# Gated linear attention and a feed-forward block on one core: three-chunk groups against units of two chunks throughout, with other paths for the rotated rows and the raw weights

## The chip, the cores and the metric

The kernel runs on one core of a Trainium2 chip. A core has a matrix engine (TensorE, "PE"; its weight loads are listed apart as "PEld"), three engines for elementwise work (VectorE "DVE", ScalarE "ACT", GpSimd "POOL"), a synchronisation engine (SyncE, "SP") that here only issues DMA transfers, and 16 DMA engines. Each engine works off its own queue of instructions in order; semaphores order the queues against each other. Matrix products land in PSUM, a separate memory; the rest of the on-chip data lies in SBUF, 128 partitions wide.

The metric is the device time of one execution in microseconds. "Span" is the time from the first to the last instruction in the profile of one execution.

## The reference

Inputs are q, k, v and complex gates `a_re + i a_im`, each of 4 batches, 8 heads, 768 steps, 48 features, then the weights of a feed-forward block. Cut to what matters:

```python
mag = sqrt(a_re**2 + a_im**2)
scale = minimum(mag, 0.999) / (mag + 1e-6)
a = (a_re + 1j*a_im) * scale
for t in range(768):                     # a state of 48 x 48 for each batch and head
    S = a[t][:, None] * S + outer(k[t], v[t])
    y[t] = q[t] @ S.real
x = y, heads side by side                # 3072 tokens x 384
xn = x / sqrt(mean(x*x) + 1e-6) * rms_g
out = (silu(xn @ w_gate) * (xn @ w_val)) @ w_out   # 384 -> 1536 -> 384
```

The weights arrive as 64-bit floats, and the kernel reads them as pairs of 32-bit words and narrows them to 32 bits itself. All products are in 32-bit floats.

## The kernel before

The 3072 tokens are 24 *chunks* of 128 steps, six to a batch. Two chunks are a *unit* (12 units); three chunks are a *group* of the feed-forward block (8 groups).

**Gates, by unit.** `gates(u)` works on tiles of 128 partitions x 768 (three blocks of 128 features by 256 steps). It takes magnitude and angle of the gates, multiplies the magnitudes up along each chunk with a scan (`p`), adds up the angles with another (`re`), takes sine (`s`) and cosine (`y`), and multiplies k by 1/p and q by p, and both by cosine and sine. The four products go into one tile `rot`. The features lie as (d, h), eight heads inside each of the 48 features, so that one head's 96 rows (48 cosine, 48 sine) are spread over the partitions. To gather them, each chunk's slice of `rot` is written to a DRAM tile `way` and read back as `kq`, 96 partitions by heads and steps (lines 629 and 631). The chunk's last decay rides along as a 129th column.

**Attention, by chunk.** `scores(n)`: eight score products `s_ps`, which VectorE masks into `am` (line 723), and eight transposes `kt_ps`, which ScalarE copies to `kt`. `finish(n)`: the state product `state_ps` and its update, the outputs `y_ps` (from `am` and v, and from q and the state before), then the norm: ScalarE squares y (line 761), VectorE scales the sum (`ssq`), GpSimd raises it to -1/2 (`rs`, line 765), ScalarE scales y to `xn` (line 767), TensorE transposes it (line 774), and VectorE writes `xT`.

**Feed-forward, by group.** For each of 12 slices of 128 hidden features: three products for gate, three for value, 384 tokens wide (line 792), Silu on ScalarE, the product `hT` on VectorE. Then for each chunk 12 products with `wo` (line 803), a copy `ot` and a DMA out.

**Weights.** There are 18 parts of 128 x 768 values: 12 of `wg` and `wv`, six of `wo`. Each is fetched raw (768 KB, line 659, on SP's queue; three buffers for the early parts, two for the others) and narrowed by one ScalarE and six VectorE operations.

**What sets the order.** The program is written as generators that are stepped by hand: while `scores` and `finish` of a chunk advance, `run(x, fill)` steps the feed-forward of the group before (the *filler*) and the gates of the unit ahead. The gate and value slices step the narrowing that they need. A list scheduler then puts the instructions of each engine's queue in an order, by their place in the program and by when it expects their inputs, and adds the semaphores; pools with few buffers make a writer wait for the readers of the buffer's last content. In the resulting order of TensorE, a chunk in the middle of the kernel stands as: 8 `s_ps`, 6 gate or value, 8 `kt_ps`, 6 gate or value, 8 `state_ps`, 16 `y_ps`, 12 gate or value, 3 `xT_ps`, 12 gate or value (hardware passes for the feed-forward are counted two to a program matmul in the profile; these are the program's).

The driver's core:

```python
for n in range(N + 1):
    ...                               # every second chunk: start gates of the unit ahead
    if n < N:
        run(scores(n), 1)
    if n > 0:
        run(finish(n - 1), 2)
    if n % GC == 0 and n:
        for _ in filler:
            pass
        ...
        filler = feed_forward(n // GC - 1, pieces, ffn)
```

Of the kernel before, what the change touches and what calls it, by code (L numbers as in the profile page):

```python
# [28 lines left out]
P = 128  # L29
# [442 lines left out]
def fast(tc, ctx, qT, kT, v, a_re, a_im, w_gate, w_val, w_out, rms_g, out, H, bad):  # L472
# [10 lines left out]
    GC = 3  # L483
# [6 lines left out]
    assert NCH % GC == 0 and NCH % UC == 0 and DM % P == 0 and D2 <= P and L * ND == D  # L490
# [23 lines left out]
    def load_gates(u):  # L514
        b, c = divmod(u * UC, NCH)
        t = UN[u]
        for name, ap in (("re", a_re), ("im", a_im)):
            t[name] = prep.tile([P, ND, T], FP32, tag=name, name=name, bufs=2)
            rows = ap[b].rearrange("(h j l) s -> j l h s", j=ND, l=L)
            queue = nc.scalar if u == 0 and name == "im" else nc.sync  # L520
            for j in range(ND):
                queue.dma_start(out=t[name][:, j], in_=rows[j][:, :, c * C:c * C + T])
        for name, ap in (("k", kT), ("q", qT)):
            t[name] = prep.tile([P, ND, T], FP32, tag=name, name=name)
            for i in range(UC):
                nc.sync.dma_start(
                    out=t[name][:, :, i * C:(i + 1) * C],
                    in_=ap[u * UC + i].rearrange("d (h t) -> (d h) t", t=C)
                                      .rearrange("(j p) t -> p j t", p=P))
        for n in range(u * UC, (u + 1) * UC):  # L530
            U[n]["v"] = unit.tile([C, H, D], FP32, tag="v", name="v", bufs=4)
            nc.sync.dma_start(out=U[n]["v"].rearrange("t h d -> t (h d)"),
                              in_=v[n * C:(n + 1) * C, :])

    rot = consts.tile([P, 4 * ND, UC, C + 1], FP32, name="rot")
    nc.vector.memset(rot[:, :, :, C:], 0.0)
    load_gates(0)

    zeros = consts.tile([P, T], FP32, name="zeros")
    nc.gpsimd.memset(zeros, 0.0)
# [17 lines left out]
    def gates(u):  # L560
# [4 lines left out]
        s, w, y, r, p = (prep.tile([P, ND, T], FP32, tag=x, name=x)  # L565
                         for x in ("s", "w", "y", "r", "p"))
# [29 lines left out]
        nc.vector.tensor_copy(  # L596
            out=rot[:, 2 * ND:, :, C].rearrange("p (a j) c -> p a j c", j=ND),
            in_=ends[:, u].unsqueeze(1).to_broadcast([P, 2, ND, UC]))
# [12 lines left out]
        for j in range(ND):  # L611
            nc.vector.tensor_tensor_scan(
                out=re[:, j], data0=im[:, j], data1=zeros, op0=ALU.add, op1=ALU.add,
                initial=UN[u - 1]["turn"][:, j] if u * UC % NCH else 0.0)
# [8 lines left out]
        for i, (x, f) in enumerate(((k, y), (k, s), (q, y), (q, s))):  # L623
            tt(rot[:, i * ND:(i + 1) * ND, :, 0:C], by_chunk(x), by_chunk(f))
        yield
        for i in range(UC):
            n = u * UC + i
            way = dram.tile([4 * DM, C + 1], FP32, tag="way", name="way")
            nc.sync.dma_start(out=way.rearrange("(r p) t -> p r t", p=P), in_=rot[:, :, i])
            to = unit.tile([D2, 2, H, C + 1], FP32, tag="kq", name="kq", bufs=3)  # L630
            nc.sync.dma_start(out=to.rearrange("d x h t -> d x (h t)"),
                              in_=way.rearrange("(x d h) t -> d x (h t)", x=2, h=H))
            U[n]["k"], U[n]["q"] = to[:, 0, :, 0:C], to[:, 1, :, 0:C]
            U[n]["decay"] = to[:, 1, :, C:]
        yield
# [10 lines left out]
    wg = consts.tile([P, ND, DF], FP32, name="wg")  # L646
    wv = consts.tile([P, ND, DF], FP32, name="wv")
# [5 lines left out]
    FW = 2 * P  # L653
    narrowed = [0]
    EARLY = 3

    def fetch(pool, to, src):
        raw = pool.tile([P, to.shape[1], 2 * to.shape[2]], I32, tag="raw", name="raw")
        nc.sync.dma_start(out=raw, in_=src)
        return raw  # L660

    def narrow(stage, to, raw):

        rows, cols = to.shape[1:]
        n = rows * cols
        words = raw.rearrange("p c f -> p (c f)").rearrange("p (n two) -> p n two", two=2)
        lo, hi = words[:, :, 0], words[:, :, 1]
        t, g = (stage.tile([P, n], I32, tag=x, name=x, bufs=1) for x in ("t", "g"))
        as_to = lambda x: x.rearrange("p (c f) -> p c f", f=cols)

        nc.scalar.activation(out=to, in_=as_to(hi.bitcast(FP32)), func=AF.Square)
        stt(as_to(g.bitcast(FP32)), to, (1.125 * 2.0 ** -15) ** 2, as_to(hi.bitcast(FP32)), ALU.is_ge)

        nc.vector.tensor_scalar(out=t, in0=g, scalar1=3, scalar2=0x3FFFFFFF,
                                op0=ALU.logical_shift_left, op1=ALU.bitwise_and)
        stt(t, g, -2 ** 30, t, ALU.bitwise_and, ALU.bitwise_or)

        nc.vector.tensor_scalar(out=g, in0=t, scalar1=-2 ** 23, scalar2=None, op0=ALU.bitwise_and)
        stt(to, as_to(lo.bitcast(U32)), 2.0 ** -52, as_to(g.bitcast(FP32)), ALU.mult)
        tt(to, as_to(t.bitcast(FP32)), to, ALU.add)  # L680

    def load_weights(early, stage):

        parts = []
        for f in range(0, DF, FW):
            parts += [(to[:, :, f:f + FW], ap, slice(0, ND), f) for to, ap in ((wg, w_gate), (wv, w_val))]
# [25 lines left out]
    def scores(n):  # L712
# [3 lines left out]
        am = u["am"] = unit.tile([C, H, C], FP32, tag="am", name="am")  # L716
        hh = H // 2
        for a in range(2):
# [4 lines left out]
            nc.vector.tensor_tensor(out=am[:, a * hh:(a + 1) * hh], in0=ps, op=ALU.mult,  # L723
# [4 lines left out]
        kt = u["kt"] = unit.tile([C, H, D2], FP32, tag="kt", name="kt")  # L728
        for a in range(2):
# [3 lines left out]
            nc.scalar.copy(out=kt[:, a * hh:(a + 1) * hh], in_=ps)  # L733
        yield

    def finish(n):
# [4 lines left out]
        if n % NCH < NCH - 1:  # L741
            ps = ps_a.tile([D2, H, D], FP32, tag="a", name="state_ps")
            for h in range(H):
                nc.tensor.matmul(ps[:, h], lhsT=u["kt"][:, h], rhs=vv[:, h], start=True, stop=True)  # L744
# [9 lines left out]
        for h in range(H):  # L754
            nc.tensor.matmul(ps[:, h], lhsT=am[:, h], rhs=vv[:, h], start=True, stop=prev is None)  # L755
# [3 lines left out]
        x = act.tile([C, DM], FP32, tag="x", name="x", bufs=1)  # L759
        ssq = act.tile([C, 1], FP32, tag="ssq", name="ssq")  # L760
        nc.scalar.activation(out=x, in_=y, func=AF.Square, accum_out=ssq)  # L761
# [4 lines left out]
        xn = act.tile([C, DM], FP32, tag="xn", name="xn")  # L766
# [13 lines left out]
    def feed_forward(g, pieces, ffn):  # L780
        xT = G[g]["xT"]
        hT = ffn.tile([P, NF, GT], FP32, tag="hT", name="hT", bufs=1)
        for f in range(NF):
            fs = slice(f * P, (f + 1) * P)
            if f * P % FW == 0:
                while narrowed[0] < 2 * (f * P // FW + 1):
                    next(pieces)
            gp = ps_g.tile([P, GT], FP32, tag="g", name="gate_ps")
            vp = ps_g.tile([P, GT], FP32, tag="g", name="val_ps")
            for p_, w_ in ((gp, wg), (vp, wv)):  # L790
                for d in range(ND):
                    nc.tensor.matmul(p_, lhsT=w_[:, d, fs], rhs=xT[:, d], start=d == 0,  # L792
                                     stop=d == ND - 1)
            sg = ffn.tile([P, GT], FP32, tag="sg", name="sg")
            nc.scalar.activation(out=sg, in_=gp, func=AF.Silu)  # L795
            tt(hT[:, f], vp, sg)
            yield
        for _ in pieces:
            pass
        for i in range(GC):  # L800
            ps = ps_g.tile([C, DM], FP32, tag="g", name="out_ps")
            for f in range(NF):
                nc.tensor.matmul(ps, lhsT=hT[:, f, i * C:(i + 1) * C], rhs=wo[:, f],  # L803
                                 start=f == 0, stop=f == NF - 1)
                if f == NF // 2:
                    yield
# [4 lines left out]
            yield  # L811


# [4 lines left out]
    for _ in gates(0):  # L818
        pass
    load_gates(1)  # L820
    filler = iter(())
    ahead = iter(())

    def run(x, fill):
        for _ in x:
            for _ in range(fill):
                next(filler, None)
            next(ahead, None)

    behind = None  # L830
    for n in range(N + 1):
        if n % UC == 0 and n // UC + 1 < NU:
            for _ in ahead:
                pass
            if n // UC + 2 < NU:
                load_gates(n // UC + 2)
            ahead = gates(n // UC + 1)
        if n % UC == 0 and n // UC + 1 == NU:
            for _ in ahead:
                pass  # L840
        if n < N:
            run(scores(n), 1)
        if n > 0:
            run(finish(n - 1), 2)
        if n % GC == 0 and n:
            for _ in filler:
                pass
            if n == GC:
                for _ in range(EARLY):
                    next(pieces)  # L850
                first.close()
                ffn = ctx.enter_context(tc.tile_pool(name="ffn", bufs=2))
            filler = feed_forward(n // GC - 1, pieces, ffn)

    ne = NU * ND * UC
    ok = act.tile([P, DM], FP32, tag="x", name="ok", bufs=1)[:, 0:2 * ne + NU]
# [12 lines left out]
    for _ in filler:  # L869
        pass  # L870
# [49 lines left out]
```

## Time and profile before

| What | Value |
| --- | --- |
| Median of 3 runs | 885.33 us (876.48 to 890.41) |
| Profiled execution | 884.13 us, span 882.3 us |
| TensorE busy | 773.3 us (88%), mean granted clock 0.939 |
| VectorE busy | 426.8 us (48%) |
| ScalarE busy | 356.2 us (40%) |
| GpSimd busy | 23.2 us (3%) |
| DMA | 81.17 MB, 36% of the 16 engines' time on SP's queue |
| First score product | 48.8 us after the start |
| TensorE's waits for `kq` from `way` | 77.3 us in 5 waits |

Busy time is the union of an engine's instructions. TensorE's overlap in a pipeline, so the distance between the starts of neighbouring matmuls says what one costs, not its listed duration. The granted clock is the share of TensorE's full clock that the throttle allowed. In the tables of groups, "idle before" is how long the engine stood still ahead of those instructions, and what ended it.

### The profile page before, as it was taken

Reading aid. Unit: us, or ns where it says so; the run is one execution under the profiler, and the core shown is the slowest. Engines: PE = TensorE matmul, PEld = TensorE weight load, DVE = VectorE, ACT = ScalarE, POOL = GpSimd, SP = SyncE. Lnnn points to the kernel's source line nnn. Section 1 sums busy time; section 2 is a strip of 40 time slices with the busy share of each in tenths; the row PEclk is TensorE's granted clock in tenths of the full one; section 3 lists DMA queues with packets and bytes.
Section 4 is the critical chain, followed back from the end, with each engine's and each line's share of the span. In section 5 each row is a group of like instructions: output and inputs, shape, how many; then the busy total and the mean of one; then the engine's idle time right before and its main releaser. Section 6 shows DMA issues by size and latency. Waiting matters only on the chain.

```text
span 882.3 us, 8797 instructions
## 1 busy us (share of the span) xinstructions
PE 773.3 (88%) x3370; PEld 530.1 (60%) x3370; DVE 426.8 (48%) x654; ACT 356.2 (40%) x520; POOL 23.2 (3%) x42
## 2 busy tenths in 40 slices
PE   0051879888879999999999999999999999999997
PEld 0051857675455566676666667666666767665554
DVE  5978768858978787768785101210121112210110
ACT  6845565643537887676783111111111111110100
POOL 1000000000000000000000000000000000000000
PEclk9995569968989999989999999999999999999999
DMA  8748374852673565482763120112111100000000
GB/s 293 154 110 201 103 169 118 202 138 72 182 186 101 114 154 156 96 189 71 137 162 73 46 63 26 29 45 55 35 29 45 43 21 1 1 9 19 1 1 30
DMA packets 85602, 81.17 MB, mean 92 GB/s; under 512 B 4144, under 2 KB 74800, under 8 KB 85552
## 3 DMA queue, kind: packets, MB, share of 16 engines
q1 hardware_dynamic: 85120, 80.13, 36.3%
q8 instruction: 28, 0.46, 0.2%
q10 hardware_dynamic: 432, 0.39, 0.1%
q14 instruction: 22, 0.18, 0.1%
HBM read 56.77 MB, written 23.74 MB: 91 GB/s over the span
## 4 chain that ended last, share of the span: by engine, by line
PE 80%; DMA 10%; DVE 6%; ACT 2%; issue 1%; SPq 1%; POOL 0%; ACTq 0%; DVEq 0%
PE val_ps L792 20%; PE gate_ps L792 20%; PE out_ps L803 19%; PE s_ps L721 6%; PE y_ps L755 5%; DMA way<-rot 4%; PE y_ps L757 4%; DMA kq<-way 4%; PE state_ps L744 3%; PE kt_ps L732 2%; DVE rot L501 1%; PE xT_ps L774 1%; DMA raw<-in_w_gate_dram 1%; DVE p L592 1%; DVE g L504 1%
## 5 line engine op out<-in xcount | busy, mean ns | idle before, releaser
L792 PE MATMUL gate_ps<-xT,wg 128*128 128x384 f32 x576 | 209.4, 501 | 5.5 <-DVE wg L501 4.8
L792 PE MATMUL val_ps<-xT,wv 128*128 128x384 f32 x576 | 207.7, 497 | 2.2 <-ACT sg L795 2.2
L803 PE MATMUL out_ps<-wo,hT 128*128 128x384 f32 x576 | 192.8, 491 | 0.2
L792 PEld LDWEIGHTS val_ps<-xT,wv 128*128 128x128 f32 x576 | 111.4, 194 | 80.1 <-issue 4.3
L501 DVE TENSOR_TENSOR hT<-val_ps,sg 128x384 f32<-128x384 f32 x96 | 53.3, 555 | 215.8 <-PE val_ps L792 200.4
L792 PEld LDWEIGHTS gate_ps<-xT,wg 128*128 128x128 f32 x576 | 109.0, 196 | 73.7 <-issue 7.9
L803 PEld LDWEIGHTS out_ps<-wo,hT 128*128 128x128 f32 x576 | 108.7, 192 | 71.7 <-issue 1.8
L721 PE MATMUL s_ps<-kq 96*128 96x128 f32 x384 | 57.2, 311 | 77.3 <-DMA kq<-way 77.3
L795 ACT ACTIVATE sg<-gate_ps 128x384 f32<-128x384 f32 x96 | 47.0, 490 | 176.6 <-PE gate_ps L792 176.2
L721 PEld LDWEIGHTS s_ps<-kq 96*128 96x128 f32 x384 | 55.5, 224 | 84.0 <-DMA kq<-way 55.6
L755 PE MATMUL y_ps<-v,am 128*128 128x48 f32 x384 | 76.0, 294 | 0.0
L757 PE MATMUL y_ps<-state,kq 96*128 96x48 f32 x320 | 68.2, 298 | 0.0
L755 PEld LDWEIGHTS y_ps<-v,am 128*128 128x128 f32 x384 | 62.9, 211 | 1.1
L723 DVE TENSOR_TENSOR am<-s_ps,causal 128x512 f32<-128x512 f32 x48 | 32.7, 688 | 51.5 <-PE s_ps L721 51.4
L761 ACT ACTIVATE x<-y_ps 128x384 f32<-128x384 f32 x24 | 11.8, 491 | 110.6 <-PE y_ps L757 101.4
L757 PEld LDWEIGHTS y_ps<-state,kq 96*128 96x128 f32 x320 | 55.1, 215 | 0.3
L808 ACT COPY ot<-out_ps 128x384 f32<-128x384 f32 x24 | 11.4, 475 | 99.3 <-PE out_ps L803 99.3
L765 POOL TENSOR_TENSOR rs<-ssq,mhalf 128x1 f32<-128x1 f32 x24 | 20.8, 867 | 754.7 <-DVE ssq L762 754.7
L733 ACT COPY kt<-kt_ps 128x384 f32<-128x384 f32 x40 | 17.6, 479 | 50.1 <-PE kt_ps L732 50.1
L744 PEld LDWEIGHTS state_ps<-v,kt 128*96 128x96 f32 x320 | 33.0, 179 | 4.4 <-issue 2.4
L744 PE MATMUL state_ps<-v,kt 128*96 128x48 f32 x320 | 32.6, 259 | 0.0
L762 DVE TENSOR_SCALAR ssq<-ssq 128x1 f32<-128x1 f32 x24 | 3.6, 152 | 58.6 <-ACT x L761 58.6
(100 smaller groups left out, 722.6 us busy)
## 6 DMA issues: line engine op xcount, KB each, us to landing
way<-rot SPq DMA_DIRECT2D x24, 774.0 KB, 8.9
kq<-way SPq DMA_DIRECT2D x24, 774.0 KB, 5.7
re<-in_a_re_dram SPq DMA_DIRECT2D x36, 128.0 KB, 2.6
k<-in_k_dram SPq DMA_DIRECT2D x24, 192.0 KB, 2.9
q<-in_q_dram SPq DMA_DIRECT2D x24, 192.0 KB, 3.3
v<-in_v_dram SPq DMA_DIRECT2D x24, 192.0 KB, 2.4
raw<-in_w_gate_dram SPq DMA_DIRECT2D x6, 768.0 KB, 8.2
raw<-in_w_val_dram SPq DMA_DIRECT2D x6, 768.0 KB, 7.0
```

The source lines that it names most:

```text
L501: nc.vector.tensor_tensor(out=o, in0=x, in1=y, op=op)
L721: nc.tensor.matmul(ps[:, h], lhsT=k[:, a * hh + h], rhs=q[:, a * hh + h], start=True, stop=True)
L723: nc.vector.tensor_tensor(out=am[:, a * hh:(a + 1) * hh], in0=ps, op=ALU.mult, in1=causal.unsqueeze(1).to_broadcast([C, hh, C]))
L732: nc.tensor.transpose(ps[:, h], k[:, a * hh + h], ident[0:D2, 0:D2])
L733: nc.scalar.copy(out=kt[:, a * hh:(a + 1) * hh], in_=ps)
L744: nc.tensor.matmul(ps[:, h], lhsT=u["kt"][:, h], rhs=vv[:, h], start=True, stop=True)
L755: nc.tensor.matmul(ps[:, h], lhsT=am[:, h], rhs=vv[:, h], start=True, stop=prev is None)
L757: nc.tensor.matmul(ps[:, h], lhsT=q[:, h], rhs=prev[:, h], start=False, stop=True)
L765: nc.gpsimd.tensor_tensor(out=rs, in0=ssq, in1=mhalf, op=ALU.pow)
L792: nc.tensor.matmul(p_, lhsT=w_[:, d, fs], rhs=xT[:, d], start=d == 0, stop=d == ND - 1)
L795: nc.scalar.activation(out=sg, in_=gp, func=AF.Silu)
L803: nc.tensor.matmul(ps, lhsT=hT[:, f, i * C:(i + 1) * C], rhs=wo[:, f], start=f == 0, stop=f == NF - 1)
```

## The change

- **Groups of two chunks.** `GC` becomes 2, so a feed-forward group is a unit: 12 groups, products 256 wide. Gate and value of a slice share one PSUM tile `gv_ps`, Silu writes straight to `hT`, and `hT` has two buffers.
- **A driver without hand-set filling.** The program is a plain sequence: gates(0), attention(0), gates(1), attention(1), the gate and value slices of groups 0 and 1 in turn (with the narrowing that they need), gates(2), attention(2), the rest of those two groups, and then for each unit gates, attention, and the feed-forward of the unit before. The interleaving is left to the scheduler. In the order that it makes, a chunk in the middle stands in TensorE's queue as: 8 `s_ps`, 8 `kt_ps`, 1 gate or value, 8 `state_ps`, 16 `y_ps`, 4 gate or value, 3 `xT_ps`; and the remaining 60 or so of the group with its 24 `out_ps` follow after the unit's second chunk.
- **Rotated rows on chip.** Instead of `rot`, `way` and `kq`, each of the four products of a unit is sent from SBUF to SBUF in three DMAs of 128 partitions to 16 partitions x 8 heads x 256 steps, into `kr` and `qr`. The decays go by a small DRAM tile `dec`.
- **Raw weights on GpSimd's queue**, with four early buffers instead of three; the narrowing works in place and needs one scratch tile less. `wg` and `wv` are laid out slice by slice.
- `am` and `kt` are two half tiles each; the squares of y are written to `xn`; `v` has three buffers instead of four; the zeros of the angle scan are a broadcast column.

The core of the diff:

```diff
-    GC = 3
+    GC = 2
...
-            U[n]["v"] = unit.tile([C, H, D], FP32, tag="v", name="v", bufs=4)
+            U[n]["v"] = unit.tile([C, H, D], FP32, tag="v", name="v", bufs=3)
...
+        dec = dram.tile([DM, UC], FP32, tag="dec", name="dec")
+        nc.sync.dma_start(out=dec.rearrange("(j p) c -> p j c", p=P), in_=ends[:, u])
+        de = unit.tile([D2, H, UC], FP32, tag="decay", name="decay", bufs=3)
+        for a in range(2):
+            nc.sync.dma_start(out=de[a * D:(a + 1) * D].rearrange("d h c -> d (h c)"),
+                              in_=dec.rearrange("(d h) c -> d (h c)", h=H))
...
-        for i, (x, f) in enumerate(((k, y), (k, s), (q, y), (q, s))):
-            tt(rot[:, i * ND:(i + 1) * ND, :, 0:C], by_chunk(x), by_chunk(f))
-        yield
+        kq = {n: unit.tile([D2, H, T], FP32, tag=n, name=n) for n in ("kr", "qr")}
+        for to, x, xs in ((kq["kr"], k, ks), (kq["qr"], q, qs)):
+            for a, (o, f) in enumerate(((xs, s), (x, y))):
+                tt(o, x, f)
+                rows = (1 - a) * D
+                for j in range(ND):
+                    nc.sync.dma_start(out=to[rows + j * L:rows + (j + 1) * L], in_=o[:, j])
+            yield
...
-            way = dram.tile([4 * DM, C + 1], FP32, tag="way", name="way")
-            nc.sync.dma_start(out=way.rearrange("(r p) t -> p r t", p=P), in_=rot[:, :, i])
-            to = unit.tile([D2, 2, H, C + 1], FP32, tag="kq", name="kq", bufs=3)
-            nc.sync.dma_start(out=to.rearrange("d x h t -> d x (h t)"),
-                              in_=way.rearrange("(x d h) t -> d x (h t)", x=2, h=H))
...
-    EARLY = 3
+    EARLY = 4
...
-        nc.sync.dma_start(out=raw, in_=src)
+        nc.gpsimd.dma_start(out=raw, in_=src)
...
         for f in range(NF):
-            gp = ps_g.tile([P, GT], FP32, tag="g", name="gate_ps")
-            vp = ps_g.tile([P, GT], FP32, tag="g", name="val_ps")
+            ps = ps_g.tile([P, 2, GT], FP32, tag="g", name="gv_ps")
...
-            sg = ffn.tile([P, GT], FP32, tag="sg", name="sg")
-            nc.scalar.activation(out=sg, in_=gp, func=AF.Silu)
-            tt(hT[:, f], vp, sg)
+            nc.scalar.activation(out=hT[:, f], in_=ps[:, 0], func=AF.Silu)
+            tt(hT[:, f], ps[:, 1], hT[:, f])
...
+    def attention(u):
+        for n in range(u * UC, (u + 1) * UC):
+            run(scores(n), finish(n))
+
+    run(gates(0))
+    attention(0)
     load_gates(1)
+    run(gates(1))
+    attention(1)
+    load_gates(2)
...
+    early = [feed_forward(g, ffn) for g in range(2)]
+    for f in range(NF):
+        while narrowed[0] < 2 * (f * P // FW + 1):
+            next(pieces)
+        for x in early:
+            next(x)
+    run(gates(2))
+    attention(2)
+    run(pieces, *early)
+    for u in range(3, NU + 1):
+        if u < NU:
+            load_gates(u)
+            run(gates(u))
+            attention(u)
+        run(feed_forward(u - 1, ffn))
```

## The prediction

> **What bounds the kernel now.** I read the busy lines and slices of the page first, then the busy time by stages, then the timeline of a dense stretch. The slices show two different kernels. For some 270 us VectorE is 70 to 90% busy and TensorE is not; from there TensorE is full to the end and VectorE falls to a tenth or two.
>
> ```profile
> PE 773.3 (88%) x3370; PEld 530.1 (60%) x3370; DVE 426.8 (48%) x654; ACT 356.2 (40%) x520; POOL 23.2 (3%) x42
> PE   0051879888879999999999999999999999999997
> DVE  5978768858978787768785101210121112210110
> ```
>
> The stages say it in microseconds (columns: window, its length, busy time and count of PE, PEld, DVE, ACT, POOL, then granted clock, DMA share, GB/s):
>
> ```profile
> 0.00:50.00 50.00, 1.21 (x5) 1.22 (x6) 37.68 (x51) 33.38 (x40) 2.36 (x18) 1.00 0.82 225
> 50.00:100.00 50.00, 26.34 (x152) 25.85 (x150) 39.66 (x59) 25.32 (x33) 1.12 (x1) 0.65 0.53 127
> ...
> 200.00:265.00 65.00, 50.97 (x224) 34.32 (x222) 55.47 (x83) 28.07 (x38) 1.28 (x2) 0.87 0.56 149
> 265.00:350.00 85.00, 83.54 (x322) 52.85 (x322) 65.12 (x95) 67.06 (x87) 3.12 (x2) 1.00 0.51 127
> 350.00:500.00 150.00, 150.00 (x675) 101.66 (x674) 100.12 (x152) 94.57 (x133) 4.78 (x5) 0.98 0.54 119
> 500.00:780.00 280.00, 280.00 (x1310) 192.20 (x1309) 47.05 (x91) 38.60 (x88) 5.28 (x10) 0.99 0.11 31
> ```
>
> So the time is TensorE's work at full clock plus what it loses. For the work I take distances between starts in a dense stretch, not mean durations, because matmuls overlap:
>
> ```profile
> 557.12 2.10 PE L792 MATMUL gate_ps<-xT,wg 128*128 128x384 f32 x6
> ...
> 559.06 2.10 PE L792 MATMUL val_ps<-xT,wv 128*128 128x384 f32 x6
> ...
> 564.86 1.95 PE L721 MATMUL s_ps<-kq 96*128 96x128 f32 x16
> ...
> 566.65 2.10 PE L792 MATMUL gate_ps<-xT,wg 128*128 128x384 f32 x6
> ```
>
> Six passes 384 wide take 559.06 - 557.12 = 1.94 us, 0.3225 each; sixteen 128 wide take 1.79 us, 0.11 each. (Each feed-forward or score matmul of the program is two passes.) The same stretch gives 0.111 for y, 0.085 for state, 0.082 for kt, 0.11 for the xT transposes. With the page's counts: 1728 x 0.3225 + 384 x 0.11 + 704 x 0.111 + 320 x 0.085 + 160 x 0.082 + 72 x 0.109 = 725.7 us. The span is 882.3, so 156.6 us are lost. After 265 us the windows show 1.5 + 5.8 us without PE work and some 7 us of clock below 1.0: 14. The other 143 us are lost in the first 265 us, where the weights are narrowed and the gates of the first units are computed on VectorE. A change helps if it shortens that stretch, and hurts if it opens holes afterwards.
>
> **The change, part by part.** *Feed-forward by two chunks.* 576 program matmuls of gate and value, 384 wide, become 864, 256 wide: 1728 passes instead of 1152. No row is 256 wide; halfway between 0.11 and 0.3225 is 0.216. 1728 x 0.216 = 373.2 against 1152 x 0.3225 = 371.5: +1.7 us. The bounds are 0 (pure proportion, 0.215) and +17 (0.01 more a pass, if a weight load of 0.11 us could not hide). Work: 727.4 us. Silu and product shrink from 0.49 and 0.56 us to about two thirds but come 144 times for 96: nothing, under PE.
>
> *Rotated rows on chip.* `way` and `kq` (two legs, 7.2 + 6.7 us in the chain of the first unit) go; 12 DMAs of 128 KB a unit come, like the `re` loads, which SP issues in about 0.61 us each and which land in 2.6. For unit 0 that is 34.6 + 12 x 0.61 + 2.6 = 44.5 us for the first score instead of 48.8. I book no gain: in the new order of VectorE's queue the first eviction of scores (`am`) stands behind all of gates(0), most of gates(1) and seven narrowed parts (near 80 us, worked out under *The start*). If that queue were short, the gain would be 4 us and twice. SP issues 15 transfers a unit where it issued 4, some 7 us of each 64; its longest waits today are for outputs to exist, so this is hidden; without that slack the next unit's loads would come 7 us late, a unit ahead of need. The small `dec`/`decay` transfers are needed one state product later and are hidden by it.
>
> [...]
>
> *Weights through GpSimd.* 18 raw loads leave SP for POOL, where `rs` (L765) waits behind them; a load that waits for its buffer holds `rs`, then `xn`, then the transpose. In the order each such load waits for a narrowing step that stands ahead of that chunk's `ssq` on VectorE anyway, so I price only lateness. A load landed in 4.3 us once the start's crowd was over and 8.2 in it; the seventh has 3.6 us of VectorE work to hide in: 4.5 us late. Bounds: none, and the 8.2 of the crowd for each of the seven that have about 6 us of cover, 7 x 3.9 = 28 if none is covered better.
>
> ```profile
> raw<-in_w_gate_dram SPq DMA_DIRECT2D x6, 768.0 KB, 8.2
> raw<-in_w_out_dram SPq DMA_DIRECT2D x6, 768.0 KB, 4.3
> ```
>
> The row says that transfers are fed well by SP. [...]
>
> *The start.* VectorE sets it. Back to back, a 768-wide operation costs 0.87 us start to start, 0.89 with dependent ones:
>
> ```profile
> 31.15 0.95 DVE L501 TENSOR_TENSOR rot<-q,y 128x768 f32<-128x768 f32 x1
> 32.02 0.95 DVE L501 TENSOR_TENSOR rot<-k,y 128x768 f32<-128x768 f32 x1
> ```
>
> In the new order its queue up to the last `xT` of group 1 holds 105 of them, and, start to start as in the same stretches, 27 `tensor_scalar`s of narrowing at 0.47, three long scans at 1.66, nine short ones at 0.66, eight `am` at 0.6, eleven PSUM reads at 0.47 and some 1.5 us of small ones: 128.6 us. It starts at 8.1 as today and waits 2 us inside gates(0). Each of the four chunks then makes it wait for scores, y, `rs` and `xT`: I take 4 us a chunk, 16 (today VectorE idles 50 - 39.7 = 10 us from 50 to 100 us, at the same half-closed clock). With the 4.5 for the weights: 8.1 + 2 + 128.6 + 16 + 4.5 = 159 us. By then TensorE has done four chunks' own work: scores 1.76, kt 0.66, state 1.36, y 3.55 (1.78 in a batch's first chunk) and xT 0.33, so 5.9 + 3 x 7.66 = 29 us: 130 lost. The pair of groups follows: 288 passes of two groups at 0.216, 62 us, while VectorE has 55 and ScalarE 41 us in its order and four PSUM buffers decouple them; I take 5 us lost (0 to 12). Unit 2's attention is filled with 48 output matmuls: 1.5. Sum 137, where today loses 143. The new order narrows first and starts the first group later, but two groups then run at once: a gain of 6 (bounds 127 and 167).
>
> *The nine units after it.* This is where I see the loss. Today 12 program matmuls of feed-forward, 24 passes or 7.7 us, stand between y and the transposes of `xn`. In the new order it is four program matmuls, 8 x 0.216 = 1.73 us, in 12 chunks of 18; five in three; eight or nine in three. The chain that they must cover:
>
> ```profile
> 575.19 0.39 PE L757 MATMUL y_ps<-state,kq 96*128 96x48 f32 x2
> ...
> 575.61 0.49 ACT L761 ACTIVATE x<-y_ps 128x384 f32<-128x384 f32 x1 [6.33 <-PE y_ps L757]
> ...
> 576.53 0.55 POOL L765 TENSOR_TENSOR rs<-ssq,mhalf 128x1 f32<-128x1 f32 x1 [25.47 <-DVE ssq L762]
> ...
> 577.12 0.58 ACT L767 ACTIVATE xn<-y_ps,rs 128x384 f32<-128x384 f32 x1 [0.92 <-POOL rs L765]
> ```
>
> From the last y to the end of `xn` it is 577.70 - 575.30 = 2.4 us with idle engines; at 100 us, with `rs` at 1.20, it was 3.1, and 3.8 at worst. Against 1.73 that leaves 0.7 to 2 us; I take 1.2, nearer the busy case: 12 x 1.2 + 3 x 0.8 = 17 us. Between kt and state stands one matmul (0.43 us) where there were six (12 passes, 3.9 us), while two kt copies take 0.48 each: 0.4 a chunk (0 to 1), 7 us. What is late next: `xT`, hence nothing but TensorE itself, which has no other work queued in between.
>
> **Sum.** 727.4 + 137 + 24 + 14 (end and clock as today) = 902.4, plus 1.8 around the span as today (884.13 - 882.3): 904 us. The profiled execution lies 1.2 us under the median of the runs, 885.33, so it stands for them. Some 2% is what a measurement here tells from no change.
>
> **Rivals.** *The start gets shorter (faster).* VectorE's waits of 20 us vanish, since its queue always holds narrowing to do, the shorter transfers show, and the pair runs without a gap; the later chain costs its lower bound, 12 x 0.7 + 3 x 0.3, and kt nothing. 904 - 20 - 5 - 15 = 864, 860 if the transfers' 4 us count too. For it: 8 to 9 tenths busy in places today. Against: in-order waits fall at the chunks, not where work is missing. It decides if the pair starts before 140 us. 0.17.
>
> *The holes are covered anyway.* VectorE and ScalarE come early to their waits and the chain is 2.4 us; 727.4 + 132 + 5 + 14 + 2 = 880. For it: TensorE loses almost nothing after 265 us today. Against: 1.73 is less than 2.4. 0.13.
>
> *Weights late.* Each of 18 loads by POOL holds ScalarE and VectorE 2 to 4 us: 904 + 36 to 72, say 950. For it: ScalarE waits 13.2 us for `raw` of `w_out` today already. 0.22.
>
> The forecast itself, 888 to 922, has 0.48; two fifths of it lie within 2% of today, under 903. Slower: 0.29 + 0.22 = 0.51; same: 0.13 + 0.19 = 0.32; faster: 0.17. With all lower bounds together the sum is 904 - 4.5 - 5 - 15 = 879, with weights and pair at their upper ones 904 + 23.5 + 7 + 15 = 950 if the holes cost 1.95 and 1 us too; the range goes a step into the rivals on both sides, 872 to 947.
>
> **What would show it.** Right: `kq` and `way` gone, the first `am` near 80 us, the pair from about 160 to 225 us, TensorE's wait for `xn` some 15 to 25 us after 270, gate passes 0.216 apart. Wrong: first `am` near 50; ScalarE waiting over 30 us for `raw`; a granted clock under 0.95 after 270, which would mean that holes cost more than their length; or no wait at `xT` at all.

## The result, and the profile after

| Kernel | Median, us | Profiled execution's span, us | Granted clock |
| --- | --- | --- | --- |
| before | 887.87 (4 runs) | 882.3 | 0.939 |
| changed | 921.64 (4 runs) | 918.4 | 0.94 |

The ratio is 1.047 (1.034 to 1.059), slower; it goes by the fast runs alone, which among the four of before are those of 876.48 and 885.33 us. The page of the changed kernel, the same three lines as of before and the line of the clock:

```profile
PE 786.3 (86%) x3946; PEld 649.4 (71%) x3946; DVE 437.2 (48%) x689; ACT 371.1 (40%) x575; POOL 32.6 (4%) x60
PE   0024806899999999999999999999999999999997
DVE  5996795795735422575462314762744021121010
PEclk9999955899798999998997999999999999989998
```

VectorE is less dense in the first third (3 to 7 tenths between the nines), and TensorE's sixth slice, 115 to 138 us, is empty. The clock row has eights and a seven far behind the start. The stages (columns as in the prediction's table; the fourth line begins about where the two first groups run):

```profile
0.00:50.00 50.00, 1.67 (x8) 1.67 (x9) 39.54 (x54) 34.04 (x41) 6.85 (x24) 1.00 0.86 209
50.00:100.00 50.00, 21.45 (x111) 20.80 (x110) 39.36 (x55) 17.37 (x23) 4.29 (x5) 1.00 0.54 111
100.00:170.00 70.00, 31.65 (x182) 29.32 (x182) 50.08 (x73) 31.54 (x43) 6.91 (x8) 0.68 0.56 127
170.00:230.00 60.00, 60.00 (x272) 52.55 (x272) 48.28 (x75) 36.95 (x53) 2.19 (x3) 0.98 0.31 72
230.00:310.00 80.00, 76.48 (x402) 60.06 (x401) 43.84 (x68) 42.03 (x64) 2.20 (x4) 0.89 0.35 71
```

The loss is again the span less the passes times their distances at full clock (gate passes at 0.216 us; a dense stretch has them 0.2158 apart): 918.4 - 727.6 = 190.8 us. Cumulated over the trace, 139.9 of them lie ahead of the pair of groups (with its first slow passes), none in the rest of it (169.7 to 231), 12.7 from there to 310 (7.2 with unit 2, up to 282, and 5.5 with the attention of unit 3), 31.3 from 310 to 850, and 6.9 at the end.

TensorE's waits (columns: total, times, longest), first over the span, then from 310 on:

```profile
PE s_ps L720 <- DMA qr<-q: 48.3, 1, 48.3
PE state_ps L745 <- ACT kt L734: 33.4, 6, 27.8
PE state_ps L745 <- DVE am L723: 27.4, 2, 25.7
PE xT_ps L774 <- ACT xn L767: 14.1, 12, 2.9
```

```profile
PE state_ps L745 <- ACT kt L734: 3.5, 3, 1.3
PE xT_ps L774 <- ACT xn L767: 3.2, 8, 0.6
```

So from 310 on TensorE stands still for only 6.7 us, and loses 31. Where the rest is, a stretch of the timeline shows (columns: start, length of the group, ...; in brackets the idle time before it):

```profile
479.57 1.03 PE L788 MATMUL gv_ps<-xT,wv 128*128 128x256 f32 x4
481.84 1.56 PE L745 MATMUL state_ps<-v,kt 128*96 128x48 f32 x16 [1.24 <-ACT kt L734]
483.24 3.29 PE L756 MATMUL y_ps<-v,am 128*128 128x48 f32 x16
486.33 1.19 PE L788 MATMUL gv_ps<-xT,wv 128*128 128x256 f32 x2
487.31 2.77 PE L788 MATMUL gv_ps<-xT,wg 128*128 128x256 f32 x6
489.87 0.76 PE L774 MATMUL xT_ps<-ident,xn 128*128 128x128 f32 x3
```

Sixteen `y` passes should take 1.78 us and take 3.09; six gate passes should take 1.29 and take 2.56. From 483.6 to 490.3 every pass costs about twice its price, and the windows say so (the last number but two is the clock):

```profile
483.00:490.50 7.50, 7.50 (x33) 6.67 (x33) 1.13 (x3) 2.72 (x5) 0.55 (x1) 0.54 0.38 77
490.50:497.00 6.50, 6.50 (x65) 6.32 (x63) 3.05 (x5) 0.86 (x2) 0.00 (x0) 1.00 0.43 65
```

Seven such spells of half clock lie between 310 and 850. With the passes partly hit they make 21 of the 31 us; holes, start to start, make 10.5. These are counts of one profiled run: over the changed kernel's four runs the granted clock went from 0.902 to 0.940.

### The profile page after: what moved, and what is told of

Same layout as the page of the kernel before. It is cut to its first block, busy times and chain, and to the rows that moved or that the text cites. A ratio compares the mean times of both kernels' runs of the same rounds, so it can differ in the third digit from the quotient of the medians.

```text
span 918.4 us, 10127 instructions
## 1 busy us (share of the span) xinstructions
PE 786.3 (86%) x3946; PEld 649.4 (71%) x3946; DVE 437.2 (48%) x689; ACT 371.1 (40%) x575; POOL 32.6 (4%) x60
## 4 chain that ended last, share of the span: by engine, by line
PE 60%; ACT 10%; DVE 7%; DMA 2%; issue 2%; POOL 1%; SPq 0%; DVEq 0%; ACTq 0%
PE gv_ps L788 31%; PE out_ps L796 13%; PE y_ps L756 5%; PE y_ps L758 4%; PE s_ps L720 3%; PE state_ps L745 2%; PE xT_ps L774 1%; ACT L790 1%; DVE p L588 1%; DVE w L504 1%; PE kt_ps L732 1%; ACT hT L790 1%; DVE re L611 1%; ACT xn L767 1%; ACT xn L762 1%
## 5 line engine op out<-in xcount | busy, mean ns | idle before, releaser
L788 PE MATMUL gv_ps<-xT,wg 128*128 128x256 f32 x864 | 224.7, 396 | 2.3 <-DVE xT L775 2.3
L788 PE MATMUL gv_ps<-xT,wv 128*128 128x256 f32 x864 | 220.5, 390 | 0.0
L788 PEld LDWEIGHTS gv_ps<-xT,wg 128*128 128x128 f32 x864 | 168.9, 199 | 26.4 <-DVE xT L775 3.1
L788 PEld LDWEIGHTS gv_ps<-xT,wv 128*128 128x128 f32 x864 | 168.5, 197 | 23.7
L501 DVE TENSOR_TENSOR hT<-gv_ps,hT 128x256 f32<-128x256 f32 x144 | 60.2, 422 | 197.4 <-ACT hT L790 197.1
L790 ACT ACTIVATE hT<-gv_ps 128x256 f32<-128x256 f32 x144 | 54.3, 382 | 193.3 <-PE gv_ps L788 192.9
L720 PE MATMUL s_ps<-qr,kr 96*128 96x128 f32 x384 | 52.3, 295 | 48.3 <-DMA qr<-q 48.3
L745 PE MATMUL state_ps<-v,kt 128*96 128x48 f32 x320 | 35.3, 266 | 60.8 <-ACT kt L734 33.4
L720 PEld LDWEIGHTS s_ps<-qr,kr 96*128 96x128 f32 x384 | 51.2, 212 | 50.8 <-DMA qr<-q 48.3
L758 PE MATMUL y_ps<-state,qr 96*128 96x48 f32 x320 | 70.2, 305 | 0.0
L758 PEld LDWEIGHTS y_ps<-state,qr 96*128 96x128 f32 x320 | 56.9, 222 | 0.0
L775 DVE TENSOR_TENSOR xT<-xT_ps,gcol 128x384 f32<-128x384 f32 x24 | 13.4, 557 | 49.4 <-PE xT_ps L774 49.4
```

The source lines that it names most:

```text
L501: nc.vector.tensor_tensor(out=o, in0=x, in1=y, op=op)
L720: nc.tensor.matmul(ps[:, h], lhsT=k[:, a * hh + h], rhs=q[:, a * hh + h], start=True, stop=True)
L745: nc.tensor.matmul(ps[:, h], lhsT=u["kt"][h * 2 // H][:, h % (H // 2)], rhs=vv[:, h], start=True, stop=True)
L758: nc.tensor.matmul(ps[:, h], lhsT=q[:, h], rhs=prev[:, h], start=False, stop=True)
L775: nc.vector.tensor_tensor(out=G[g]["xT"][:, :, i * C:(i + 1) * C], in0=ps, op=ALU.mult, in1=gcol.unsqueeze(2).to_broadcast([P, ND, C]))
L788: nc.tensor.matmul(ps[:, i], lhsT=w_[:, f * P // FW, d, cols], rhs=xT[:, d], start=d == 0, stop=d == ND - 1)
```

## The experiments

Ratios are to the kernel before, run on the same chip in turn; its medians there were 892 to 897 us, so ratios compare better than microseconds between tables.

| Run | Median, us | Ratio (95% interval) | Span, us |
| --- | --- | --- | --- |
| e1_fill | 911.58 | 1.021 (1.013 to 1.029) | 902.4 |
| e2_raw_sp | 883.92 | 0.986 (0.976 to 0.996) | 888.4 |
| e3_spare_narrow | 1007.02 | 1.128 (1.119 to 1.137) | 999.2 |
| e4_spare_wide | 959.19 | 1.073 (1.061 to 1.084) | 954.2 |
| e5_pool_hold | 912.06 | 1.019 (1.009 to 1.028) | 911.8 |
| e6_best_k4 | 872.81 | 0.975 (0.965 to 0.985) | 871.5 |
| e7_best_k2 | 884.55 | 0.988 (0.977 to 0.999) | 883.4 |
| e8_before_onchip | 910.29 | 1.014 (1.001 to 1.027) | 908.5 |
| e9_spread | 867.47 | 0.972 (0.964 to 0.980) | 868.3 |
| e10_before_pool | 915.89 | 1.027 (1.016 to 1.037) | 915.7 |
| e11_sequence | 891.39 | 1.000 (0.996 to 1.004) | 896.3 |
| e12_spread_pool | 868.62 | 0.965 (0.955 to 0.976) | 864.0 |

**Filling by hand, and what halves the clock.** The first run puts the feed-forward back between the steps of the attention:

```diff
     for u in range(3, NU + 1):
-        ...
-            attention(u)
-        run(feed_forward(u - 1, ffn))
+        filler = feed_forward(u - 1, ffn)
+        ahead = gates(u + 1)                       # while there is one
+        for n in range(u * UC, (u + 1) * UC):
+            for x, fill in ((scores(n), 1), (finish(n), 2)):
+                for _ in x:
+                    for _ in range(fill):
+                        next(filler, None)
+                    next(ahead, None)
+        run(ahead, filler)
```

> From unit 3 on, the feed-forward of the unit before is stepped by hand inside the attention (one slice after scores, one after kt, two after y, two after xT; a slice is six matmuls, 2.6 us), and the gates of a unit are written one unit ahead. Nothing else differs from the changed kernel. Theory A (thin filler: TensorE's holes of some 15 us behind kt and y after 228 us, and the half-clock spells of some 25 us around the attention, cost the time): both nearly vanish from unit 3 on, the holes under 3 us, the spells at most 3; 921.6 - 9 - 20 = about 892 us (885 to 902). Theory B (the loss is in the weights and the start): nothing to gain here, 915 to 928 us.

It took 16 us off the span (10 between the medians, 2.6% by the ratios), about half of what was expected. Holes behind 225 us fell from 14.7 to 7.7 us (three of 0.8 to 1.5 us are left from unit 3 on); but half clock still cost 23.7 us there, after 29.9. Theory B is out; of theory A the part on holes stands and the part on the clock does not: covering the holes did not keep the clock here (0.97 granted from 265 to 850 us, 0.96 in the changed kernel).

Two runs ask what does. Each adds the same time of passes in the places of the holes, narrow or wide:

```diff
+    def spare(n):                                  # behind kt, and behind the norm of y; from unit 3 on
+        ps = ps_a.tile([C, H, D], FP32, tag="a", name="spare_ps")
+        for h in range(H):
+            nc.tensor.matmul(ps[:, h], lhsT=ident, rhs=U[n]["v"][:, h], start=True, stop=True)
```

```diff
+        ps = ps_a.tile([C, FW], FP32, tag="a", name="spare_ps")
+        for _ in range(4):
+            nc.tensor.matmul(ps, lhsT=ident, rhs=wg[:, 0, 0], start=True, stop=True)
```

> In units 3 to 11, 8 spare matmuls 48 wide (16 passes of 0.111, 1.78 us) stand between kt and state and behind y; their result is used by nothing. 33 such blocks are 58.7 us of added passes, and they cover the holes. Theory A (the clock halves for lack of work in the array, and 48-wide passes are little work): as many half-clock spells as the changed kernel has after 228 us (9) or more, so about 921.6 + 58.7 - 10 (holes) + 0 to 15 = 970 to 985 us. Theory B (the clock halves because of the holes): the spells go too, 921.6 + 58.7 - 10 - 20 = 950 us.

> As the run with narrow spare matmuls, but each block is 4 matmuls 256 wide (8 passes of 0.2155, 1.72 us; 33 blocks are 57 us). Theory A (array work decides the clock): the half-clock spells mostly vanish (at most 3 after 228 us), 921.6 + 57 - 10 - 17 = 952 us, and some 20 us or more under the narrow one. Theory B (holes decide): the same as the narrow one within 6 us, 945 to 953.

The narrow one is 48 us slower than the wide one, with 1.7 us more of added passes. The same window of the changed kernel, of the narrow run and of the wide one:

```profile
265.00:850.00 585.00, 576.62 (x2967) 473.59 (x2966) 236.06 (x391) 226.97 (x373) 11.22 (x18) 0.96 0.26 52
```

```profile
265.00:850.00 585.00, 580.57 (x3077) 491.57 (x3076) 223.08 (x361) 223.35 (x351) 10.77 (x16) 0.92 0.27 52
```

```profile
265.00:850.00 585.00, 578.12 (x3054) 478.05 (x3053) 229.50 (x377) 219.45 (x356) 11.64 (x17) 0.99 0.27 52
```

TensorE is busy to the same 578 to 581 us in the two runs, and the clock is 0.92 in one and 0.99 in the other: half clock costs 55.0 us after 228 in the narrow run, 13.5 in the wide one. That is theory A: in these two runs the clock did not go by TensorE's busy time but by what the added passes were. Sixteen passes 48 wide in a place, one each 0.11 us, left it at 0.92; eight 256 wide, of about the same time, had it at 0.99. The narrow run came out above its expectation (970 to 985), since the spells grew more than was allowed for.

The changed kernel shows the same with nothing added. Of its seven spells from 310 on, six begin after 3.4 us (as long as the shortest spells) in which TensorE never stood still and had little but `state` and `y` passes, all 48 wide, to do (two gate passes at most); the seventh, at 483.6, has the hole of 1.24 us in that time. The spell at 551.8, and the window before it, which holds `y` passes alone but for the tail of `state`:

```profile
548.40:551.80 3.40, 3.40 (x34) 3.40 (x32) 1.11 (x2) 0.00 (x0) 0.00 (x0) 1.00 0.00 0
551.80:555.30 3.50, 3.50 (x11) 2.95 (x11) 0.15 (x1) 1.16 (x3) 0.55 (x1) 0.51 0.43 124
```

Among the runs described below, e6 and e9 have eleven more such spells from 310 on, none of them behind a hole. A chunk's 16 `state` and up to 32 `y` passes stand in one piece, 4.9 us long. They do so in the kernel before as well, whose profiled run has only two spells between 310 and 850 (at 389.1 and 668.9); why it met fewer no run settles, and no run broke the piece up.

**The queue of the raw loads.**

```diff
-        nc.gpsimd.dma_start(out=raw, in_=src)
+        nc.sync.dma_start(out=raw, in_=src)
```

> The 18 raw weight loads are issued by SP again, as in the kernel before; all else as changed. Theory A (the queue of the raw loads costs little, since TensorE's loss before 228 us comes from VectorE's work in order): 915 to 928 us, the pair of groups starts within 5 us of 170. Theory B (weights late through GpSimd): ScalarE's waits for raw (29 us before 172 us) fall by half or more, the pair starts 10 to 25 us earlier, 895 to 912 us. A third reading: SP waits 38 us in all for v's buffer before 232 us, and raw loads queued behind that come later still: 925 to 945 us.

One line gives back 30 us of span (38 between the medians), and the kernel is then 1.4% under before (0.976 to 0.996). Theory A, mine, is wrong on that. The loss ahead of the pair is 119.1 us instead of 139.9, and the pair starts at 147.7. But the transfers are not what is faster: behind the start's crowd a raw load takes 4.6 to 5.3 us through GpSimd and 4.5 to 6.7 through SP. What differs is VectorE's order. Counted in the trace, 81 narrowing operations stand ahead of the fourth chunk's `xT` in the changed kernel, 49 with the loads on SP; 32 x 0.83 = 26.6 us. Presumably the scheduler expects the loads to be there sooner on a queue of their own, and so puts more narrowing ahead of the first chunks; no run shows its reckoning. The first eviction of scores, changed and on SP:

```profile
78.25 0.68 DVE L723 TENSOR_TENSOR am<-s_ps,causal 128x512 f32<-128x512 f32 x1
```

```profile
70.39 0.68 DVE L723 TENSOR_TENSOR am<-s_ps,causal 128x512 f32<-128x512 f32 x1
```

To tell order from lateness, the next run keeps GpSimd's queue and holds the order by hand:

```diff
-                narrow(stage, to, raws.pop(i))
+                with tc.issue_after(G[1]["last"].ins) if i >= 7 else ExitStack():   # chunk 3's xT
+                    narrow(stage, to, raws.pop(i))
```

> The raw loads stay on GpSimd's queue as changed, but VectorE's narrowing from the eighth of the 18 parts on is queued behind the xT of the fourth chunk, which is about the order that VectorE had in the run with the loads on SP (49 narrowing operations ahead of that xT, against 81 in the changed kernel). Theory A (the loss by GpSimd's queue is one of order: 32 operations, 26.6 us, of narrowing moved ahead of the first four chunks): the pair of groups starts at 145 to 155 us instead of 170, and the time is 885 to 900 us. Theory B (the transfers themselves come late through GpSimd): 912 to 930 us, the pair at 165 or later.

Neither: the time is theory B's lower edge, the start of the pair theory A's. Ahead of the pair the loss fell to 118.6 us and the pair started at 148.6, as theory A has it. But some 16 us were lost again between 210 and 245: narrowing `wo` now falls together with unit 2's attention. ScalarE's and TensorE's waits from 205 to 260:

```profile
ACT wo L670 <- DMA raw<-in_w_out_dram: 5.9, 2, 3.1
```

```profile
PE state_ps L746 <- ACT kt L735: 7.5, 1, 7.5
```

ScalarE stands at a raw load with the copy of `kt` queued behind, and TensorE waits for that copy, in a spell of half clock afterwards (mean granted clock of the run 0.913, 0.940 in the changed kernel). So order explains the start, and the run does not clear the transfers. The last run below does.

The queue alone on the kernel before:

```diff
-        nc.sync.dma_start(out=raw, in_=src)        # kernel before
+        nc.gpsimd.dma_start(out=raw, in_=src)
```

> The kernel before, with the 18 raw loads on GpSimd's queue alone. VectorE's order stays near (37 narrowing operations ahead of the fourth xT, 43 before). Theory A (in the changed kernel the queue cost its time by order, the transfers themselves are fed as well): 880 to 897 us beside 888. Theory B (GpSimd's transfers are late, 2 us or more for each of 18): 910 to 930 us.

2.7% slower, with nearly the same order: theory B's size. The landings are longer there (median us from issue, last column; before: 8.2, 7.0 and 4.3):

```profile
raw<-in_w_gate_dram POOLq DMA_DIRECT2D x6, 768.0 KB, 10.2
raw<-in_w_val_dram POOLq DMA_DIRECT2D x6, 768.0 KB, 10.0
raw<-in_w_out_dram POOLq DMA_DIRECT2D x6, 768.0 KB, 4.9
```

Five loads behind the start took 10.6 to 15.5 us. In that kernel `way` and `kq` still travel; in the changed one they do not. The loss is 13 us greater by 275 us and another 20 behind, nearly all of it half clock (0.88 granted from 265 to 350 us and 0.94 from 350 to 500, where before has 1.00 and 0.98). Whether the late loads or what else moved in the order makes the 20 stays open.

**The rotated rows alone.** The kernel before with this change's `kr`, `qr` and `dec`:

> The kernel before, with this change's path for the rotated rows alone (SBUF to SBUF, decays by a small DRAM tile, three buffers of v). As the prediction has it, nothing is gained: 880 to 897 us beside a before of 888. Rival (the two legs by DRAM are on the path in each of the first four units): TensorE's waits for kq, 77 us, fall by 8 or more, 865 to 879 us. Other side: SP's 15 transfers a unit for 4 come late, 898 to 912.

```diff
-            nc.sync.dma_start(out=way..., in_=rot[:, :, i])
-            nc.sync.dma_start(out=to..., in_=way...)
+                for j in range(ND):
+                    nc.sync.dma_start(out=to[rows + j * L:rows + (j + 1) * L], in_=o[:, j])
```

Slower by 1.4% (0.1 to 2.7), within the third reading. The first score is at 48.7 us, where it was, and waits for scores are 74.6 us for 77.3. What came on top are waits for weights, 13.4 for `wv`, 10.1 for `wo` and 3.3 for `wg`, where there were 4.8 at `wg`: 30 narrowing operations stand ahead of the fourth `xT` for 43. So the order moved here too; whether that or SP's longer queue makes the loss, no run separates.

**Fewer parts ahead.** The raw loads on SP, the hand filling, and four or two parts of narrowing ahead of the fourth chunk (the hold above with 4 or 2 for 7):

> Raw loads on SP, the feed-forward stepped by hand inside the attention from unit 3 on, gates one unit ahead, and only four parts of narrowing ahead of the fourth chunk's xT. From the run on SP (884) take the gain of the hand filling (921.6 - 911.6 = 10 to 15) and up to 3 parts x 7 operations x 0.83 = 17 us of VectorE's queue: 855 to 872 us if VectorE's idle time under the pair (some 45% of 62 us in the run on SP) takes the moved work. If the pair is then bound by VectorE, nothing comes of the last term: 868 to 880.

> As the one before with two parts ahead in place of four, so another 11 us of VectorE's queue behind the fourth chunk. Theory A (idle time of VectorE under the pair takes it): 845 to 865 us. Theory B (the pair waits for weights): the same as with four within 6 us, and TensorE waits more than 10 us for wg or wv.

Four parts: 872.8, just above the first reading and inside the second. The pair starts at 135.6 and loses some 6 us, so VectorE's idle time under it does take most of the moved work. Two parts: 12 us slower, though the pair starts earlier still: the wait only moved on, as unit 2's attention falls into the pair's second half and TensorE then waits for `am` and `wo` (3.5 and 4.3 us) and drops to half clock there (mean granted clock of the run 0.932, 0.959 with four parts). Neither reading has that; it is not the wait for `wg` and `wv` of theory B (2.4 us).

> The kernel with four parts of narrowing ahead (872.8 us), with more feed-forward stepped inside the attention: two slices behind kt instead of one, three behind y instead of two, and the output products in halves, so that all of a unit's feed-forward lies between attention steps. The earlier run still lost some 17 us after 250 us to half-clock spells. Theory A (a spell comes when a few us of attention are diluted too little): spells after 250 us fall from 11 to 5 or fewer, 860 to 868 us. Theory B (dilution beyond covering the holes changes nothing): 870 to 877 us.

```diff
-            for x, fill in ((scores(n), 1), (finish(n), 2)):
+            for x, fills in ((scores(n), (1, 2)), (finish(n), (3, 2))):
...
+                if f == NF // 2 - 1:
+                    yield                           # out_ps in halves
```

867.5, at the upper edge of theory A's range. Spells after 250 us fell to four, as theory A has it, but from seven: the eleven of the expectation were too many. And the cost of half clock behind 240 fell from 17.6 to 13.1 us. The span's 3.2 us agree in sign with theory A; against e6 alone the intervals overlap.

> The run with the raw loads on SP (884 us, profiled span 888), with the first two feed-forward groups one after the other instead of in turn. Theory A (side by side halves the rate at which the pair asks for weights): group 0 asks for two parts each 5.2 us while narrowing two takes VectorE 11.2 us, so TensorE waits for wg and wv, 20 us or more: 900 to 925 us. Theory B (seven parts are narrowed ahead, so it hardly matters): 878 to 895 us.

```diff
-        for x in early:
-            next(x)
+    for x in early:                                # the whole of group 0, then group 1
+        for f in range(NF):
+            ...
+            next(x)
```

Theory B in size: 7.5 us slower than side by side, with 10.3 us of waits for `wg`. That is what the pair is worth once the narrowing is not all ahead.

> The kernel of the run with spread filling (867.5 us), with the raw loads on GpSimd's queue. VectorE's order ahead of the fourth xT is held the same by hand: 24 narrowing operations. Theory A (in the changed kernel the queue cost by the order that the list scheduler made of it): 866 to 876 us. Theory B (loads through GpSimd come late by themselves, as in the kernel before with GpSimd's queue alone, +24 us): 885 to 895 us.

The same kernel as e9 with the loads on GpSimd: 868.6, ratio 0.965 beside 0.972. With VectorE's order held, the queue costs nothing that these intervals show in this kernel. TensorE's waits in it:

```profile
PE s_ps L720 <- DMA qr<-q: 48.3, 1, 48.3
PE xT_ps L775 <- ACT xn L768: 11.1, 4, 2.8
PE state_ps L746 <- DVE am L724: 8.3, 1, 8.3
PE state_ps L746 <- ACT kt L735: 6.9, 1, 6.9
```

Beside the changed kernel, the waits for `am` and `kt` are 15 us instead of 61. Both e9 and e12 beat both kernels: 2.8 and 3.5% under before, and by the ratios (0.972 and 0.965 to 1.047) 7 to 8% under the changed one.

## Why the prediction was right, and where not

It said slower, 904 us with a range of 872 to 947; it is 921.6, at the upper end of the forecast's own range (888 to 922). Term by term, in the profiled execution:

| Term | Predicted, us | Measured, us |
| --- | --- | --- |
| TensorE's work | 727.4 | 727.6 |
| lost ahead of the pair | 130 | 139.9 |
| lost in the pair | 5 | 0 |
| lost in unit 2 | 1.5 | 7.2 |
| lost in the nine units, holes and clock, and at the end | 24 + 14 | 5.5 + 31.3 + 6.9 |

- *The work.* 0.2158 us a pass: right.
- *The start.* The first `am` came at 78.3 (near 80 was said), the pair at 169.7 for 159. VectorE's queue was as long as worked out. The term that was mis-sized is the 4 us of waiting in each chunk: its waits for scores, state, `ssq` and `xT` are 2.4 + 5.5 + 14.6 + 4.0 = 26.5 us, 6.6 a chunk, since `y` runs at half clock in three of the four chunks (passes 0.213 us apart, 0.111 in the fourth; the trace's record of the clock begins at 111.5 us) and two of the four `ssq` waits are 5.1 and 5.2 us. VectorE's waits before 172 us:

```profile
DVE ssq L763 <- ACT xn L762: 14.6, 4, 5.2
DVE state L501 <- PE state_ps L745: 5.5, 4, 2.2
DVE xT L775 <- PE xT_ps L774: 4.0, 3, 1.6
DVE am L723 <- PE s_ps L720: 2.4, 3, 1.2
```

- *The first score.* 48.3 where 44.5 was worked out: the issues ended where they should (41.1), but the last six pieces landed in 5.9 to 7.8 us, not in 2.6 like `re`. That no gain was booked was right, and e8 agrees. The crowd of the start is not the reason: the twelve pieces land one every 1.04 us, while SP issues one every 0.65, and at 421 us, with hardly anything else to move, they land 1.04 us apart again. The later a piece of such a batch, the longer it takes. Median us from issue to landing, last column, from 33 to 50 us and from 420.8 to 430.5:

```profile
qr<-qs SPq DMA_DIRECT2D x3, 128.0 KB, 6.3
qr<-q SPq DMA_DIRECT2D x3, 128.0 KB, 7.7
```

```profile
qr<-qs SPq DMA_DIRECT2D x3, 128.0 KB, 4.5
qr<-q SPq DMA_DIRECT2D x3, 128.0 KB, 5.7
```

- *Weights through GpSimd.* 4.5 us of lateness was the wrong kind of price. Lateness was little (e12). But the queue set the order, and with it some 21 us of the start (e2, e5). The sum held all the same, as the queue of VectorE had been counted in the order as it was; what I failed to see is that this order hung on the queue, and that undoing this one line would have made the change a gain. The rival "weights late" is not what happened: ScalarE's waits for `raw` were 17.5 + 9.3 + 6.6 = 33.4 us, over my own mark of 30, yet e12 has the loads on the same queue and loses nothing by it. GpSimd's issuing was not what cost either: the 18 issues took 0.72 to 0.91 us each, the eight with VectorE busy from their start to their end 0.72 to 0.78, the seven with VectorE idle 0.72 to 0.91.
- *Unit 2.* I called it filled with 48 output products. Most of them (34) stand behind its attention: up to 282 us a hole of 1.8 us at `state_ps`, and some 5 us of half clock.
- *The nine units.* 24 us for holes and 7 for the clock were forecast, 31; from 310 on 10.5 and 21 came, and unit 3 had lost 5.5 before that, 37 in all. The sum came near by luck: `y` to `xT` cost 0.54 to 0.75 in a hole, about my lower bound of 0.7, as the chain took its idle time (GpSimd's `rs` took 0.55 us in the 18 of 24 chunks where VectorE stood still beside it for most of that time or all of it, and 0.79 to 1.27 in the other six), and where the filler ran at half clock it covered the chain (eight passes from 486.3 to 489.9 us, 3.5 us). The wait for `xn` was 3.2 us from 310 on where 15 to 25 was said. The mark that came nearest was the granted clock from 265 on, 0.96 where before had 0.99; it stayed above the 0.95 that I had named, although the clock cost twice what the holes did.
- *The range.* The upper sum adds 15 us for holes of 1.95 and 1 us; 12 x 0.75 + 18 x 0.6 are 20. Nothing above hangs on it.

## What to carry to other kernels

A list scheduler turns any edit into an edit of the order: compare the order on the busiest engine part by part, and ask of each part what the order would be without it. When a kernel loses more than its gaps, take distances between starts of equal passes, and look whether they double, as six gate passes did here (2.56 us for 1.29). Look for long pieces of narrow passes (here 3.4 us with little but passes 48 wide ahead of six spells of seven), and not only for gaps; that wide passes inside such a piece would keep the clock was not tried here.

## What the runs showed of the hardware that was not expected

Most spells of half clock in the changed kernel from 310 on lasted 6.8 us by the granted clock in the trace (418.73 to 425.56, 483.58 to 490.41, 497.24 to 504.06, 616.71 to 623.53, 807.85 to 814.68), two half of that (551.85 to 555.26, 691.80 to 695.21), and their starts lie at multiples of some 3.413 us from the first: 64.85 = 19 x 3.413, 78.51 = 23 x 3.413, 133.12 = 39 x 3.413, 197.98 = 58 x 3.413, 273.07 = 80 x 3.413, 389.12 = 114 x 3.413.

Work without a gap did not keep the clock here: six of these seven spells began with no hole in the 3.4 us before them, and the run with narrow passes had TensorE idle for only 4.4 of the 585 us from 265 to 850 with 0.92 granted, where the one with wide passes had it idle for 6.9 with 0.99.

How much work of TensorE keeps the clock was not measured: e9's filling, as dense in time as e6's (TensorE busy for 585.0 and 584.4 of the 585 us from 265 to 850), still met four spells; it leaves the piece of `state` and `y` whole.
